# A fused convolution and gated MLP in fp32: four of six block pairs in the Strassen form instead of three, with a new order of all engines

## The chip, the cores and the metric

The kernel runs on one core of one Trainium2 chip. The core has a matrix engine (TensorE, PE in the profile, with its weight loads shown apart as PEld), three engines for elementwise work (VectorE or DVE, ScalarE or ACT, GpSimd or POOL), a sync engine (SyncE or SP) that here only issues DMAs, and 16 DMA engines that move data between the memory of the chip (HBM) and the on-chip memory. ACT issues DMAs too, on a queue of its own. Each engine runs its own list of instructions in order, and waits for the others through semaphores. The matrix engine writes into eight accumulation banks (PSUM). The metric is the time of one execution in microseconds (us); lower is better.

## The reference

The input is x, 8 sequences of 4096 tokens with 192 channels, in fp32. First comes a causal depthwise convolution with 7 taps. The taps are shared by the channels of a head (8 heads of 24 channels) and normalised by a softmax. Its output is the input of an MLP:

```python
rms = np.sqrt(np.mean(x * x, axis=-1, keepdims=True) + 1e-06)
xn = x / rms * rms_g
g = xn @ w_gate                              # 32768 x 192 @ 192 x 1536
val = xn @ w_val                             # 32768 x 192 @ 192 x 1536
return (g / (1 + np.exp(-g)) * val) @ w_out  # 32768 x 1536 @ 1536 x 192
```

Nearly all arithmetic lies in the three matrix products.

## The kernel before

**Tiling.** The 32768 tokens are cut into 32 pairs of 2 x 512 tokens (`PAIRS`, T = 512). The 1536 inner channels are 12 blocks of 128, taken two at a time as block pairs j = 0 to 5 (`NP`). The 192 input channels are three thirds of 64 rows. One matmul uses half of the PE rows: the gate product runs in one half while the value product runs in the other.

**Gate and value products.** For one block pair and one token pair there are four results, a to d (2 token tiles x 2 blocks). In the plain form each is the sum of three thirds, called A, B and E, so 12 products (Aa, Ba, Ea, Ab and so on). In the Strassen form the first two thirds are taken as a 2 x 2 x 2 product with seven multiplications (P1 to P7), and the last third adds Q1 to Q4: 11 products. The tuple `FORM` says which block pairs use which. Each product is three matmul passes, for operands cut into a high part, a low part and a combination, times two halves, so six matmuls of 512 columns (line 899). The seven Strassen products need additions between them. These are done on the banks: f1 copies bank a, when it holds P1 alone, to bank b; f3 copies P5 from bank c to a buffer; f4 adds the buffer to bank b and writes c; f5 adds it to b after P7 and writes d. The copies are at lines 667 (ACT) and 669 (DVE), the adds at line 967 (DVE). So P6 and P2 wait for f1; P7, Q2 and P3 wait for f4; Q4, Q3 and P4 wait for f5.

**Silu and multiply.** When a result is complete, ACT takes the silu of the gate half into a buffer (ga to gd, line 973), and DVE multiplies it with the value half into a tile (ma to md, line 980). Then the double bank is free again; there are four of them. `open` takes the next free one.

**Output product.** It too is a Strassen form, over all six block pairs: seven multiplications o1 to o7, one step per block pair (o1.0 to o7.5, 42 steps, line 923). They add up in three banks X, Y and Z; o1 starts X, o7 starts Z, Y is a copy of X (c1). The sums h1 to h4 of the multiplied tiles (line 950, DVE or POOL) feed o5, o7, o6 and o3. At the end DVE and ACT combine the banks (s7, c2, C21, C22) and transpose them (T11 to T22, line 938), and stores go out (st, line 1022).

**The next tokens.** Beside this work the tokens of the following pairs are made ready: loads (ld, line 146), seven taps (cv0 on ACT, cv1 to cv6 on DVE, line 435), square, reduction, factor, spread and scaling (sq, red, pow, bc, mul; pow and mul on POOL), eight puts into a scratch in HBM (pl, line 1033), six fetches from it with the channels across partitions (ft, line 631), sums for the Strassen form (x1 to x4, line 827) and the cuts into parts (n, l, d, lines 667, 813 and 815).

**Weights.** The parts of the weights lie in HBM (`wd`) and are loaded into a ring of ten slots, one piece of 192 KB at a time (line 785, from SP). A plain block pair needs six pieces, a Strassen one nine. When the last product that uses a piece is written down, `ring_load` loads the next piece into its slot.

**What sets the order.** The order is written out by hand as words; no scheduler changes it. `LINE` lists the PE steps of one token pair (a word such as P1.0 is product P1 of block pair 0). `ORDER` lists, for one window, what all engines are told: `p3` is the next three PE steps, `Vma.0` is DVE doing ma of block pair 0; the first letter is the engine (A, V, G for POOL, S for SP). A `+` means the next token pair, `++` the one after, `-` the one before. `FIRST` is the window of token pair 1, which still uses unsplit weights, with the preparation of the split weights (W) beside it. The last lines of the function run them:

```python
run([w for row in FIRST for w in row.split()], 1)
for w in range(2, PAIRS + 1):
    run([w for row in ORDER for w in row.split()], w)
```

Of the kernel before, what the change touches and what calls it, by code (L numbers as in the profile page):

```python
# [1323 lines left out]
```

## Time and profile before

| | us |
|---|---|
| three runs | 2497.64, 2503.84, 2503.82 (median 2503.82) |
| the profiled execution | 2498.01 |
| its span, first to last instruction | 2496.2 |
| PE busy | 2477.4 (99%) |
| DVE busy | 2013.4 (81%) |
| ACT busy | 926.6 (37%) |
| POOL busy | 852.5 (34%) |
| gate products, line 899 | 12420 matmuls, 1442.9 busy |
| adds f4 and f5, line 967 | 180, 1229 ns each |
| silus, line 973 | 744, 598 ns each |
| multiplies, line 980 | 744, 684 ns each |
| ring loads, line 785 | 1350 of 192 KB |
| HBM | 349.26 MB read, 58.39 MB written |

The profile is one execution. A row gives the line, the engine, the operation and its tiles, then the busy time. An idle time before an instruction is put down to what ended it. The ends of matmuls are modelled, so that a busy PE can still have short pauses between steps. The chain that ended last follows the work back from the last instruction: at each step to what released it, or to the instruction before it on its engine. The two kinds of stretches of one token pair look different: in a stretch of gate products (828.23 to 872.19) the DMA engines are busy at 0.81 and move 212 GB/s, and DVE is busy 33.76 of 43.96 us; in a stretch of output steps (872.19 to 896.90) it is 0.48, 108 GB/s, and 21.85 of 24.71 us. The granted PE clock is 1.00 in both.

### The profile page before, as it was taken

How to read it: one execution, taken by the hardware profiler on the slowest of the kernel's cores; microseconds unless marked ns; L12 is line 12 of the kernel's file. 1: busy time of each engine (PE TensorE's matmuls, PEld its weight loads, DVE VectorE, ACT ScalarE, POOL GpSimd, SP SyncE). 2: the span in 40 equal slices, each digit the busy share in tenths (PEclk: the TensorE clock that was granted, in tenths of full speed). 3: DMA queues.
4: the chain of work that ended last, by engine and by line, in shares of the span. 5: the costliest groups of instructions: out<-in, count | busy, mean ns of one | idle time of the engine just before them, and what ended most of it. 6: DMA issues, size and time to landing. Idle time of an engine off the chain costs nothing.

```text
span 2496.2 us, 69094 instructions
## 1 busy us (share of the span) xinstructions
PE 2477.4 (99%) x29140; PEld 1932.4 (77%) x29140; DVE 2013.4 (81%) x2482; ACT 926.6 (37%) x1349; POOL 852.5 (34%) x640
## 2 busy tenths in 40 slices
PE   8999999999999999999999999999999999999999
PEld 5647778877777787777877788777777877778887
DVE  8668888788878788878888788888787888888864
ACT  6443334333333333333333343333333333333331
POOL 0553333423243324343333333233433233333331
PEclk9999999999999999999999999999999999999999
DMA  7365667766678666677666677666686666786652
GB/s 150 59 189 152 155 170 192 173 180 157 156 171 205 169 166 158 160 180 193 172 160 157 168 192 176 179 154 157 170 201 172 165 158 162 181 197 171 159 140 81
DMA packets 701735, 412.22 MB, mean 165 GB/s; under 512 B 506610, under 2 KB 687730, under 8 KB 701426
## 3 DMA queue, kind: packets, MB, share of 16 engines
q1 hardware_dynamic: 540176, 353.65, 56.1%
q10 hardware_dynamic: 161250, 54.16, 9.7%
q8 instruction: 230, 3.77, 0.6%
q14 instruction: 79, 0.65, 0.1%
HBM read 349.26 MB, written 58.39 MB: 163 GB/s over the span
## 4 chain that ended last, share of the span: by engine, by line
PE 96%; DMA 2%; SPq 1%; DVE 0%; ACT 0%; issue 0%; ACTq 0%; DVEq 0%
PE ps L899 56%; PE ps L923 34%; PE ps L871 2%; PE ps L1070 2%; DMA xb<-xd 1%; PE ps L1111 1%; SPq L146 0%; SPq L229 0%; DMA ht<-in_moe_w_gate_dram 0%; DMA x<-in_x_dram 0%; DMA ht<-in_moe_w_val_dram 0%; ACT tt L973 0%; DVE ht L980 0%; SPq L631 0%; ACT o_sb L1119 0%
## 5 line engine op out<-in xcount | busy, mean ns | idle before, releaser
L899 PE MATMUL ps<-part,ring 64*128 64x512 f32 x12420 | 1442.9, 389 | 0.0
L899 PEld LDWEIGHTS ps<-part,ring 64*128 64x128 f32 x12420 | 1185.8, 184 | 236.5 <-issue 18.0
L973 ACT ACTIVATE tt<-ps 128x512 f32<-128x512 f32 x744 | 430.9, 598 | 726.4 <-PE ps L899 586.4
L980 DVE TENSOR_TENSOR ht<-ps,tt 128x512 f32<-128x512 f32 x744 | 495.5, 684 | 190.5 <-ACT tt L973 185.3
L923 PE MATMUL ps<-ht,wo_sb 128*32 128x384 f32 (+2 forms) x6696 | 443.1, 380 | 3.3 <-DVE ht L980 3.3
L923 PE MATMUL ps<-ht,x 128*32 128x256 f32 (+2 forms) x6696 | 441.9, 379 | 0.0
L950 POOL TENSOR_TENSOR ht<-ht 128x512 f32<-128x512 f32 x186 | 283.7, 1538 | 433.3 <-PE ps L923 377.1
L950 POOL TENSOR_TENSOR hs<-ht 128x512 f32<-128x512 f32 x93 | 120.2, 1293 | 834.2 <-DVE ht L980 832.3
L923 PEld LDWEIGHTS ps<-ht,wo_sb 128*32 128x32 f32 x6696 | 296.2, 110 | 121.9 <-issue 21.5
L923 PEld LDWEIGHTS ps<-ht,x 128*32 128x32 f32 x6696 | 302.5, 110 | 90.6
L435 DVE SCALAR_TENSOR_TENSOR y<-xh,tp,y 128x1536 f32<-128x1536 f32 x186 | 342.5, 1841 | 1.3
L667 ACT COPY ps<-ps 128x384 f32<-128x384 f32 (+1 forms) x121 | 104.1, 860 | 408.7 <-PE ps L899 311.7
L967 DVE TENSOR_TENSOR ps<-ps,tt 128x1024 f32<-128x1024 f32 x180 | 221.3, 1229 | 42.1 <-PE ps L899 35.0
L667 ACT COPY tt<-ps 128x384 f32<-128x384 f32 (+1 forms) x122 | 91.0, 746 | 227.0 <-PE ps L923 207.8
L923 PE MATMUL ps<-hs,x 128*32 128x128 f32 (+2 forms) x2232 | 161.0, 379 | 0.0
L950 DVE TENSOR_TENSOR ht<-ht 128x512 f32<-128x512 f32 x186 | 126.5, 693 | 8.0 <-POOL hs L950 4.6
L923 PEld LDWEIGHTS ps<-hs,x 128*32 128x32 f32 x2232 | 108.9, 110 | 27.7
L667 ACT CAST part<-xb 128x1024 fp32r<-128x1024 f32 x87 | 91.3, 1050 | 104.0 <-DMA xb<-xd 67.1
L950 DVE TENSOR_TENSOR ht<-hs,ht 128x512 f32<-128x512 f32 x155 | 122.4, 806 | 2.9 <-PE ps L923 1.1
L950 DVE TENSOR_TENSOR hs<-ht 128x512 f32<-128x512 f32 x93 | 116.4, 1252 | 2.1
L815 DVE SCALAR_TENSOR_TENSOR part<-part,xb 128x1024 fp32r<-128x1024 f32 x87 | 105.5, 1213 | 0.0
L813 DVE TENSOR_TENSOR part<-xb,part 128x1024 fp32r<-128x1024 f32 x87 | 105.4, 1212 | 0.0
(136 smaller groups left out, 1460.1 us busy)
## 6 DMA issues: line engine op xcount, KB each, us to landing
ring<-wd SPq DMA_DIRECT2D x1350, 192.0 KB
xb<-xd SPq DMA_DIRECT2D x122, 256.0 KB
xd<-xh ACTq DMA_DIRECT2D x240, 96.0 KB
xh<-in_x_dram SPq DMA_DIRECT2D x192, 105.0 KB
xb<-xd ACTq DMA_DIRECT2D x58, 256.0 KB
out_dram<-o_sb ACTq DMA_DIRECT2D x93, 96.0 KB
wd<-part SPq DMA_DIRECT2D x5, 1152.0 KB
xh<-in_x_dram SPq DMA_DIRECT2D x56, 98.4 KB
```

The source lines that it names most:

```text
L435: nc.vector.scalar_tensor_tensor(out=y, in0=xk, scalar=w, in1=y, op0=ALU.mult, op1=ALU.add)
L667: nc.scalar.copy(out=dst, in_=src)
L813: e.tensor_tensor(out=split_of(g, 1).bitcast(F32R), in0=src, in1=high, op=ALU.subtract)
L815: nc.vector.scalar_tensor_tensor(out=split_of(g, 2).bitcast(F32R), in0=high, scalar=1.0 + SPLIT, in1=src, op0=ALU.mult, op1=ALU.subtract,)
L871: nc.tensor.matmul(out=self.both(j, c)[:, h, :], lhsT=wf[HALF[h], k, 2 * j + f, :], rhs=rb[HALF[h], k, g, :], start=(k == 0), stop=(k == K ...
L899: nc.tensor.matmul(out=self.both(j, c)[:, h, :], lhsT=left[HALF[h]], rhs=right[HALF[h]], start=(first and q == 0), stop=True, skip_group_c ...
L923: nc.tensor.matmul(out=self.acc(b)[i * Q : (i + 1) * Q, at : at + n], lhsT=left, rhs=cols, start=fresh, stop=True, skip_group_check=True, ...
L950: engine[eng].tensor_tensor(out=dst, in0=a, in1=b, op=op)
L967: nc.vector.tensor_tensor(out=self.both(j, c), in0=self.both(j, "b"), in1=s5, op=ALU.add)
L973: nc.scalar.activation(out=tt[:, t, :], in_=self.both(j, c)[:, 0, :], func=AF.Silu)
L980: nc.vector.tensor_tensor(out=self.hv(j, "abcd".index(c)), in0=self.both(j, c)[:, 1, :], in1=tt[:, t, :], op=ALU.mult,)
L1070: nc.tensor.matmul(out=bank(h, bks[h])[:], lhsT=wf[HALF[h], AT[h][k], u * NF + f, :], rhs=xb[HALF[h], g, k, :], start=(k == 0), stop=(k == ...
```

## The change

`FORM` becomes (0, 1, 1, 0, 1, 1): block pairs 1, 2, 4 and 5 are in the Strassen form, 0 and 3 plain (before: 0, 2 and 4 in the Strassen form). `LINE`, `ORDER` and `FIRST` are replaced. Per window there are 68 gate products for 69 and 48 ring loads for 45. Four f4 and four f5 stand for three each; f1 is three times on ACT and once on DVE (before three on ACT), f3 four times on ACT (before two on ACT, one on DVE). The eight puts and two of the six fetches move from ACT's queue to SP's. Between DVE and POOL some h sums, x3 and some l cuts change places. All PE steps of a token pair now lie in its own window, so that no step of two token pairs interleaves. No instruction changes in kind or size, and nothing outside of these four constants is edited; the lines below them move by three.

```diff
--- before.py
+++ after.py
@@ -68,46 +68,49 @@
     SPAN = 1509
     SPLIT = 2.0**-12
     HIGH = 0xFFFFF000
-    FORM = (1, 0, 1, 0, 1, 0)
+    FORM = (0, 1, 1, 0, 1, 1)
     PLAIN = tuple((j, c) for j in range(NP) for c in "abcd")
     ORDER = (
-        "Vd.0 An.4 An.3 Ac2- p5- Gh4.2- Vl.2 Vd.4 Vh4.3- Vl.3 Vd.3 Vl.0 Vd.2 Vh4.0- Vh4.5-",
-        "p8- Gh4.4- Gh4.1- VT11- VC22- p2- p1 Gl.4 Acv0+ Af1.0 VT22- VC21- p1- VT21- p3 Vcv1+",
-        "p1 Af3.0 Ast1.2- Vcv2+ Vf4.0 p3- p3 Aga.0 Ast1.0- Vcv3+ VT12- Vma.0 Sst0.2- Agc.0",
-        "Ast0.3- p1 Vf5.0 p2 Vcv4+ p1 Vmc.0 Vcv5+ p2 Sst1.3- p1 Sst0.4- Sst0.0- Agb.0 Ast1.1-",
-        "Agc.1 Ast0.1- Vmb.0 p2 Vcv6+ Agd.0 p2 Aga.1 Vmd.0 Vma.1 Vmc.1 p1 Asq+ Vred+ p1 Af1.2",
-        "Sst1.4- Gh1.0 Agb.1 Vmb.1 p1 Gpow+ p3 Af3.2 p1 Vf4.2 p4 Aga.2 Agd.1 Vma.2 Vbc+ Vf5.2",
-        "Gmul+ p1 Agc.2 p1 Apl.0+ Apl.1+ Apl.2+ p1 Vmd.1 Vmc.2 p6 Agd.2 Agb.2 Apl.3+ Vmb.2",
-        "Vmd.2 Apl.4+ p1 Agb.3 Aga.3 Apl.5+ p1 Vmb.3 Vma.3 p4 Af1.4 Vf3.4 Agc.3 Apl.6+ Apl.7+",
-        "p3 Vmc.3 p1 Vf4.4 p2 Aga.4 Gh1.1 p1 Agd.3 Aft.0+ Sft.2+ Vma.4 Vf5.4 Vh3.1 Sft.3+",
-        "Aft.1+ Sld.0++ Vmd.3 Sft.4+ Sld.1++ Sft.5+ Sld.2++ Sld.3++ Sld.4++ Sld.5++ Sld.6++",
-        "Sld.7++ p7 Gh1.3 Agc.4 Agd.4 Vmc.4 Vmd.4 Agb.4 p1 Vh1.2 Vh3.0 Vmb.4 p7 An.0+ p1",
-        "Aga.5 Agd.5 p1 Vh1.4 An.1+ Vx1+ Vmd.5 Vma.5 p1 Gh3.3 p2 Gh3.2 Agb.5 p2 Gh3.4 p2 Gx3+",
-        "Agc.5 Vd.1+ p1 Vh2.0 Vmc.5 Vh2.1 Vmb.5 Vh1.5 Vh2.2 Vh3.5 Vl.1+ Vh2.5 Vh2.4 Ac1 p1",
-        "Gx2+ An.2+ p6 Gh2.3 Gx4+ As7 p8",
+        "p2 Ast0.0- Sst0.4- Ast1.3- Sst0.2- Sst0.3- Sst1.4- p6 Sst0.1- Aga.0 Vma.0 Vcv4+ p3",
+        "Agc.0 Agd.0 Ast1.1- Vmc.0 p3 Vmd.0 Vcv5+ Ast1.0- Agb.3 Vmb.3 Af1.1 p2 Agb.0 Vcv6+",
+        "Vmb.0 p1 Af3.1 p3 Vf4.1 Aga.1 p2 Vma.1 p2 Vf5.1 p4 Asq+ Ast1.2- Aga.3 Vred+ Agd.1",
+        "Vmd.1 Vma.3 p1 Agc.1 Af1.2 p1 Agb.1 Vmc.1 p1 Gpow+ p1 Vbc+ Vmb.1 Gmul+ p1 Af3.2 p2",
+        "Spl.0+ Spl.1+ Aga.2 Vf4.2 p1 Spl.2+ Vma.2 p2 Vf5.2 p3 Spl.3+ Spl.4+ Agc.2 Agd.2",
+        "Spl.5+ Agb.2 Vmc.2 Vmd.2 p3 Vmb.2 Spl.6+ Spl.7+ Af1.4 p3 Agc.3 Af3.4 Vmc.3 p2 Aga.4",
+        "Vf4.4 Vma.4 p5 Sft.2+ Vf5.4 p1 Agd.3 Vmd.3 Sft.3+ Sft.0+ Sft.1+ p1 Agc.4 Vmc.4",
+        "Sft.4+ Sld.0++ Agd.4 Sft.5+ Sld.1++ Sld.2++ Sld.3++ Vmd.4 Sld.4++ Sld.5++ Sld.6++",
+        "Sld.7++ p3 Af3.5 Vf1.5 p1 Agb.4 Vf4.5 Vmb.4 p2 Aga.5 Vh1.4 Vma.5 p3 Gh1.1 Gh1.0",
+        "Gh1.2 Gh3.0 Gh1.3 Gh3.1 Gh3.3 Vf5.5 p3 Vh2.3 Vh3.2 Vh2.2 Gh3.4 p3 An.0+ Agb.5 Agd.5",
+        "Vx1+ p2 Vx3+ Vmd.5 Gx2+ Vl.0+ Vh2.4 Vmb.5 p1 Vh1.5 Vh3.5 p4 Agc.5 Ac1 An.1+ An.2+",
+        "An.3+ Gx4+ Gh2.1 p9 Vmc.5 Vh2.5 As7 An.4+ p2 Vh2.0 Vd.3+ Gl.2+ p3 Ac2 p4 Acv0++ p2",
+        "Gh4.1 Gh4.2 Gl.1+ Vh4.0 Vh4.5 Vd.4+ Vd.2+ Vl.3+ Vh4.4 Vh4.3 p6 Vl.4+ VT11 Vd.1+ VC22",
+        "Vd.0+ VC21 VT22 VT21 Vcv1++ p6 VT12 Vcv2++ Vcv3++",
     )
     FIRST = (
         "p1 Vcv5+ W p2 Vcv6+ p1 Aga.0 Vma.0 p2 Asq+ W W p1 Agb.0 W Vmb.0 W p1 Vred+ p2 Agc.0",
-        "Vmc.0 W p1 Gpow+ W W W p1 W p1 Agd.0 W Vmd.0 p1 Vbc+ Gh1.0 p1 Gmul+ p1 Aga.1 Vh3.0 W",
-        "Vma.1 p1 W W W W p1 W p1 Agb.1 Apl.0+ Vmb.1 p1 Apl.1+ p1 Apl.2+ W p1 Agc.1 Apl.3+ W",
-        "W W Vmc.1 Apl.4+ p1 W W Apl.5+ p1 Apl.6+ p1 Agd.1 Apl.7+ Vmd.1 p1 Gh1.1 W p1 W W W",
-        "p1 Aga.2 Vh3.1 W Vma.2 W p3 Agb.2 Vmb.2 W p1 W W W p1 W p1 Agc.2 W Vmc.2 p3 Agd.2 W",
-        "Vmd.2 p1 W W W Vh1.2 W p1 W p1 Aga.3 Gh3.2 Vma.3 p2 W p1 Agb.3 W W W Vmb.3 p1 W W p1",
-        "Aft.0+ p1 Aft.1+ Agc.3 Sft.2+ Vmc.3 p1 Sft.3+ W p1 Sft.4+ W W W Sft.5+ p1 Agd.3 W",
+        "Vmc.0 W p1 Gpow+ W W W p1 W p1 Agd.0 W Vmd.0 p1 Vbc+ Gh1.0 p1 Gmul+ p1 Aga.1 Gh3.0 W",
+        "Vma.1 p1 W W W W p1 W p1 Agb.1 Spl.0+ Vmb.1 p1 Spl.1+ p1 Spl.2+ W p1 Agc.1 Spl.3+ W",
+        "W W Vmc.1 Spl.4+ p1 W W Spl.5+ p1 Spl.6+ p1 Agd.1 Spl.7+ Vmd.1 p1 Gh1.1 W p1 W W W",
+        "p1 Aga.2 Gh3.1 W Vma.2 W p3 Agb.2 Vmb.2 W p1 W W W p1 W p1 Agc.2 W Vmc.2 p3 Agd.2 W",
+        "Vmd.2 p1 W W W Gh1.2 W p1 W p1 Aga.3 Vh3.2 Vma.3 p2 W p1 Agb.3 W W W Vmb.3 p1 W W p1",
+        "Sft.0+ p1 Sft.1+ Agc.3 Sft.2+ Vmc.3 p1 Sft.3+ W p1 Sft.4+ W W W Sft.5+ p1 Agd.3 W",
         "Vmd.3 W p1 Gh1.3 p2 Aga.4 Gh3.3 Vma.4 W p1 W W p1 W p1 Agb.4 W Vmb.4 p3 Agc.4 W",
-        "Vmc.4 p1 W p2 Agd.4 An.1+ Vmd.4 p1 Vx1+ Sld.0++ Vh1.4 p1 Gx3+ Vd.1+ p1 Aga.5 Gh3.4",
-        "Vma.5 Vl.1+ Sld.1++ p1 Gx2+ p1 An.2+ p1 Agb.5 Sld.2++ Gx4+ Vmb.5 p1 Sld.3++ p2 Agc.5",
-        "Sld.4++ Vmc.5 p1 Sld.5++ p1 Sld.6++ Agd.5 p1 An.0+ Vmd.5 p1 Vh2.0 Sld.7++ Vh1.5 p2",
-        "Gh2.3 Vh3.5 Vh2.5 p1 Vh2.1 p1 Vh2.4 p1 Ac1 Vh2.2 p2 R p7 As7 p7",
+        "Vmc.4 p1 W p2 Agd.4 Vx1+ Vmd.4 p1 Vx3+ Vh1.4 p1 Gx2+ p1 Aga.5 Gh3.4 Vma.5 An.1+",
+        "Sld.0++ p1 An.2+ p1 An.3+ p1 Agb.5 Sld.1++ Gx4+ Vmb.5 p1 An.4+ Sld.2++ p1 Vd.3+ p1",
+        "Gl.2+ Agc.5 Sld.3++ Vmc.5 Gl.1+ p1 Sld.4++ Vd.4+ p1 Vd.2+ Agd.5 Sld.5++ p1 Vl.3+",
+        "An.0+ Vl.0+ Vmd.5 Vd.0+ p1 Vh2.0 Sld.6++ Vl.4+ Vh1.5 p1 Vh2.3 Vd.1+ Sld.7++ p1 Vh3.5",
+        "Vh2.5 p1 Vh2.2 p1 Vh2.4 p3 Ac1 Gh2.1 R p3 Vh4.0 p1 Vh4.4 p1 Vh4.3 p1 Gh4.2 p5 As7 p1",
+        "Vh4.5 p4 Ac2 p2 Acv0++ p3 VT11 Gh4.1 p5 VC22 p2 VC21 p3 Vcv1++ p2 VT12 VT22 VT21",
+        "Vcv2++ Vcv3++",
     )
     LINE = (
-        "P1.0 P5.0 P6.0 P2.0 Q1.0 P7.0 P3.0 Q2.0 Ac.1 Q4.0 Q3.0 P4.0 Bc.1 Ec.1 Aa.1 Ba.1 Ea.1",
-        "Ab.1 Eb.1 P1.2 Bb.1 P5.2 P6.2 P2.2 Q1.2 Ad.1 Ed.1 P7.2 P3.2 Bd.1 Q2.2 Q3.2 Q4.2 Aa.3",
-        "Ba.3 P4.2 Ea.3 Ab.3 Bb.3 Eb.3 Ac.3 Bc.3 P1.4 P5.4 Ec.3 P6.4 P2.4 Q1.4 Ad.3 Bd.3 P7.4",
-        "Ed.3 Q2.4 P3.4 Q4.4 P4.4 Ad.5 Q3.4 Ed.5 Aa.5 Ea.5 Ab.5 Bd.5 Ac.5 Bc.5 Ba.5 Bb.5 Ec.5",
-        "Eb.5 o1.0 o1.5 o1.3 o1.1 o1.4 o1.2 o7.0 o7.3 o7.4 o2.0 o7.1 o7.2 o2.5 o6.0 o7.5 o6.2",
-        "o2.3 o6.1 o2.4 o6.4 o6.3 o6.5 o4.4 o2.1 o4.1 o5.0 o2.2 o5.5 o4.3 o5.3 o4.5 o5.2 o5.4",
-        "o5.1 o4.2 o4.0 o3.5 o3.2 o3.3 o3.1 o3.4 o3.0",
+        "Aa.0 Ea.0 Ad.0 Ac.0 Ba.0 Ed.0 Bd.0 Ec.0 Bc.0 Ab.3 P1.1 Bb.3 Eb.3 Ab.0 Eb.0 Bb.0 P5.1",
+        "P6.1 P2.1 Q1.1 Aa.3 P7.1 Ba.3 Ea.3 Q4.1 P3.1 Q2.1 Q3.1 P1.2 P4.1 P5.2 P6.2 P2.2 Q1.2",
+        "Ac.3 P7.2 Q2.2 P3.2 Q4.2 P4.2 Q3.2 P1.4 Ec.3 Bc.3 P2.4 P5.4 P6.4 Q1.4 Ad.3 Ed.3 P7.4",
+        "Bd.3 Q2.4 P3.4 Q4.4 P1.5 P4.4 P5.5 Q3.4 P6.5 P2.5 Q1.5 Q2.5 P7.5 o1.0 o1.3 o1.5 o1.2",
+        "Q3.5 Q4.5 P4.5 P3.5 o1.4 o7.0 o7.1 o1.1 o7.4 o7.2 o2.0 o2.4 o2.3 o2.2 o7.3 o6.1 o6.4",
+        "o6.2 o7.5 o2.5 o6.3 o4.0 o6.0 o6.5 o4.5 o4.4 o5.2 o5.3 o2.1 o4.1 o5.4 o5.5 o5.1 o5.0",
+        "o4.3 o4.2 o3.0 o3.4 o3.3 o3.1 o3.5 o3.2",
     )
 
     cst = ctx.enter_context(tc.tile_pool(name="cst", bufs=1))
```

## The prediction

> **What bounds the kernel now.** I read the page's busy row first, then the chain that ended last, one window of that chain in order of time, and only then the groups, the waits and the timeline of the engines that feed TensorE (PE).
>
> ```profile
> PE 2477.4 (99%) x29140; PEld 1932.4 (77%) x29140; DVE 2013.4 (81%) x2482; ACT 926.6 (37%) x1349; POOL 852.5 (34%) x640
> PE 96%; DMA 2%; SPq 1%; DVE 0%; ACT 0%; issue 0%; ACTq 0%; DVEq 0%
> ```
>
> PE is the bound, and 96% of the chain is PE following PE. But a busy share of 99% cannot show a stall of some tenths of a us, so I measure PE by the pace of its steps. One window of the chain (columns: start, length, what):
>
> ```profile
> 752.65 44.03 PE ps L899 x381
> 796.68 24.84 PE ps L923 x304
> 821.52 0.89 PE ps L899 x6
> 822.41 0.79 PE ps L923 x8
> 823.20 2.94 PE ps L899 x24
> 826.14 2.09 PE ps L923 x24
> ```
>
> These six runs are one token pair: 64, 1 and 4 gate products (6 matmuls each) and 38, 1 and 3 output steps (8 rows each). A gate product costs (44.03 - 0.89) / 63 = 0.685 us, and 0.89 - 0.685 = 0.205 us is paid once per run. An output step costs (24.84 - 0.79) / 37 = 0.650 us, and 0.14 once per run. The other runs fit: 4 x 0.685 + 0.205 = 2.945 against 2.94, 3 x 0.65 + 0.14 = 2.09. So a window is 75.58 us, and no stall above 0.1 us hides in it. It happens 30 times (12420 / 414 gate matmuls): 2267 of the 2496 us.
>
> The rows that decide what a shorter round trip costs (timeline; the wait before it in brackets) and the two waits of the weight loads:
>
> ```profile
> 844.38 1.23 DVE L967 TENSOR_TENSOR ps<-ps,tt 128x1024 f32<-128x1024 f32 x1 [0.43 <-PE ps L899]
> 854.58 1.00 ACT L667 COPY ps<-ps 128x1024 f32<-128x1024 f32 x1 [0.95 <-PE ps L899]
> 870.26 1.09 ACT L973 ACTIVATE tt<-ps 128x512 f32<-128x512 f32 x2 [0.76 <-PE ps L899]
> 871.38 1.29 DVE L980 TENSOR_TENSOR ht<-ps,tt 128x512 f32<-128x512 f32 x2 [1.38 <-ACT tt L973]
> ...
> PEld ps L899 <- DVE ht L980: 6.4, 30, 0.2
> PEld ps L899 <- ACT ps L667: 4.8, 30, 0.3
> ```
>
> The ACT copy at 854.58 is f1 of block pair 4. Between P1.4, which it reads, and P6.4, which needs it, stand two products, 2 x 0.685 = 1.37 us. The copy takes 1.00, and the next weight load waits about 0.16 us for it (4.8 / 30) without PE losing pace. So both hand-overs together (PE to the copy, the copy to PE) take at most 1.37 - 1.00 = 0.37 us. The DVE add at 844.38 starts 0.20 after the product it waits for by the pace above (23 products after 828.23 + 0.205, 844.19), and the multiply that starts at 871.38 ends near 872.06, the output step that needs it starts at 872.19, 0.12 later. So both together are 0.32 to 0.37 us. Two products are thus enough for a copy on ACT, and just so; the old order never gives a DVE add fewer than three (P7.4 Ed.3 Q2.4 P3.4 Q4.4).
>
> **The change part by part.** The sum is made against the profiled execution, 2498.01 us (span 2496.2, 1.8 around it). The three timed runs are 2497.64, 2503.84 and 2503.82, so it lies 5.8 us below their median.
>
> 1. Four pairs in the Strassen form: 4 x 11 + 2 x 12 = 68 products instead of 69, output steps stay 42. Saves 0.685 x 30 = 20.5 us, on the path because PE is the path.
>
> 2. Fewer runs. The new line goes 64 products (all but the last four), four output steps (o1.0 o1.3 o1.5 o1.2), four products (Q3.5 Q4.5 P4.5 P3.5), 38 steps, and the windows no longer interleave: two runs of each kind instead of three. Saves (0.205 + 0.14) x 30 = 10.3 us.
>
> 3. Three DVE adds now have only two products between what they read and what needs them: P7.1 Ba.3 Ea.3 Q4.1, P7.2 Q2.2 P3.2 Q4.2, P6.5 P2.5 Q1.5 Q2.5. The add takes 1.23 (its 180 rows lie at 1.23), with hand-overs 1.55 to 1.60, against 1.37: a stall of 0.18 to 0.23 even with DVE idle before it. Lower end 0.10 (the smallest hand-overs that fit these rows, 0.20 + 0.04); I take 0.20, as the weight load of the ACT copy shows almost no reserve. 3 x 0.20 x 30 = 18 us (9 to 21).
>
> 4. The first step of the second output sum. o7.0 opens the bank that held d of pair 5 and must wait for multiply md.5. PE does Q4.5, P4.5, P3.5, o1.4, o7.0. ACT has gb.5 ahead of gd.5, and gb.5 needs P4.5. From the end of P4.5: hand-over 0.12 to 0.20, two silus 1.09, 0.03 to the multiply, 0.68, 0.12 to PE: 2.07. PE has P3.5, a run change and o1.4 to do: 0.685 + 0.14 + 0.65 = 1.475. Stall 0.60, x 30 = 18 us. Lower end 0.5. Upper end 1.1: x1 and x3 stand on DVE ahead of md.5 and wait for the fetched tokens; in the trace x1 waits 1.87 us a window (54.2 / 29). I stay at 0.60: the fetch is issued about 10 us earlier in the gate phase than before.
>
> 5. Smaller ones: f1.5 is now on DVE (a copy of this size took 1.23 there) behind md.4, with three products to run in; md.1 stands behind the 2.2 us reduction. Together 0.1 a window, 3 us (0 to 9).
>
> 6. Other engines. DVE gains two adds (2.46), one split of a token sum (1.21) and x3 (1.22), loses one h1 (1.25) and two splits of fetched tokens (2.42), trades one h3 for one h4: +1.2 us in 75, to about 83% busy, hidden by the PE time beside it except at 3 to 5. POOL +1.9 (h1 1.29 and h3 1.54 in, h4 1.54 and x3 1.74 out, one more split of 2.38), ACT two more copies (2.0) and ten DMA issues fewer: both below half busy, no cost. If that cover went, the o-phase of DVE (21.85 busy of 24.71 before) would be first.
>
> 7. SP. Eight puts and two fetches move from ACT's queue to SP, and three more weight pieces are loaded (48 for 45, 30 x 3 x 192 KB = 17 MB on 412). In the old line the shortest time between a freed ring slot and its use is six products, 4.1 us, without a wait for it; in the new line it is seven (4.8), and eight (5.5) where puts stand between, two ahead of one load at most at 0.59 us each in the trace: 5.5 - 1.2 = 4.3. I cost it at nothing; without that margin every late load stalls PE one for one.
>
> 8. The ends. All ten stores of the last pair now stand behind the last transpose; in the trace eight stores took 6.72 us on ACT's queue and about half of these had started before. +3 us (0 to 5). The start moves the same puts behind the weight writes of SP: 0, from -4 to +4.
>
> Sum: 2498.0 - 20.5 - 10.3 + 18 + 18 + 3 + 3 = 2509.2 against the profiled 2498.0, that is +11. Counted from the median it is 2515; the runs of before fall at both levels, so I forecast the middle, **2512 us**.
>
> The page "DMA: Bandwidth & Descriptors" of the Trainium skill (Anatomy of one DMA) gives about 2.0 us plus bytes over 436 GB/s; a ring piece would land in an estimated 2.5 us. By it, part 7 keeps an estimated 1.8 us (4.3 - 2.5) and rival B would have half its chance, with the sum as it is; the trace bounds the landing only from above, at 4.1 us.
>
> **The rivals.**
>
> A. The gain stands, other side: the round trip of DVE is shorter than I say, or PE takes up the waits in its queue as it did the 0.16 us of the copy, and parts 3 and 5 go to nothing, while the wait at o7.0 is at most 0.2. For it: PE lost no pace at the copy. Against: the add is 0.23 longer than the copy. Then 2498 - 30.8 + 3 + 0 to 6 = 2470 to 2477; it turns at 1.02 us of stalls a window, and up to there the result stays below 2501. Chance 0.26, with mixed cases up to 2492.
>
> B. SP becomes the bound: the puts wait for the normalisation on POOL, and ring loads behind them come late. For it: DMA engines are at 0.81 in the gate phase. Against: part 7. One us late at one place of each window adds 30 us: 2540. Chance 0.12.
>
> C. The granted clock falls because PE now pauses five times a window. The stretches of this trace show a granted clock of 1.00, the last one (2380 to 2496) 0.98; 2% on 30 x 74.6 us is 45 us: 2555. Against: no pause is above 1.1 us. Chance 0.03. The Trainium skill, "TensorE: Matmul & The Clock Gate", A second HAM failure mode, says that short pauses between groups of matmuls can make the gate swing; this trace has no such pauses and can't show it.
>
> My forecast (stalls of 1.0 to 1.9 us a window) has 0.59 and a range of its own of 2500 to 2530.
>
> **How the numbers follow.** About 0.3% (7.5 us) can be told from no change here. The forecast's 0.59 gives 0.46 slower and 0.13 same; A gives 0.23 faster and 0.03 same; B and C are slower, 0.15. Faster 0.23, same 0.16, slower 0.61. The range of 8 in 10 cuts the lowest part of A and the far part of B and C: 2476 to 2536.
>
> **What would show it.** In the chain, runs of 64, 4, 4 and 38, a first run longer than 44.03 by about 0.7 us, and the run that starts with o1.4 longer than 24.84 by 0.6. In the waits, weight loads of L902 waiting for the DVE add at L970 about 90 times, and loads of L926 for the multiply at L983 about 0.6 us or more 30 times. Waits for ring loads would mean B; a first run near 44.0 would mean A. The part I am least sure of is 4: were the bank free earlier, 18 us go.

## The result: 56 us slower, and where the time is

The changed kernel takes 2559.61 us (median of four runs, 2559.06 to 2561.63); the kernel before took 2503.32 beside it. The ratio is 1.0232, with a 95% interval of 1.0214 to 1.0249. The forecast was 2512, in a range of 2476 to 2536: the direction was right, the size was not. The profiled execution took 2559.58 us, its span is 2557.8.

The busy row and the chain of the changed kernel's page, which answer to the two lines shown of the kernel before:

```profile
PE 2496.4 (98%) x28960; PEld 1921.2 (75%) x28960; DVE 2114.0 (83%) x2511; ACT 989.8 (39%) x1409; POOL 957.6 (37%) x671
PE 86%; DVE 5%; DMA 3%; ACT 2%; issue 2%; POOL 1%; SPq 1%; ACTq 0%; DVEq 0%; POOLq 0%
```

PE still is the bound, but its share of the chain falls from 96% to 86%: the other engines now stand on the path. One window of the chain (start, length, what; "issue" is time in which nothing in the profile explains the wait):

```profile
1006.21 16.73 PE ps L902 x144
1022.94 0.14 issue
1023.08 9.89 PE ps L902 x84
1032.97 0.13 issue
1033.10 14.62 PE ps L902 x126
1047.72 0.13 issue
1047.86 2.33 PE ps L902 x18
...
1050.20 1.65 PE ps L902 x10
1051.85 2.75 PE ps L926 x32
1054.60 2.29 PE ps L902 x16
...
1056.96 1.09 ACT tt L976 x2
...
1058.08 0.70 DVE ht L983
...
1058.92 24.26 PE ps L926 x296
```

The runs of 64, 4, 4 and 38 are there, but the 64 products are cut into 24, 14, 21, 3 and 2. What each piece takes beyond 0.685 us a product (and 0.205 for the change of kind at the start) shows what the cuts cost: 0.23, 0.43, 0.37, 0.28 and 0.28, together 1.59 us, or 0.40 for each of the four cuts if all of it is put down to them. The cuts lie ahead of Q4.1, Q4.2, P6.5 and Q2.5. After the four products, the silus and the multiply lead to o7.0: from 1054.60 to 1058.92 it is 4.32 us, against 3.735 for the work of PE in it, a pause of 0.59, and the run of 37 steps behind it takes 0.21 more than 37 x 0.65. So the window is 76.96 us, 2.4 above 74.55, what 68 products, 42 steps and two changes of kind each way cost without a pause.

Between the two profiled spans lie 61.6 us: 30 windows of 77.16 on average instead of 75.73 (42.9; most are 77.0 and 75.6), a start that is 15.9 longer (below), and 2.6 at the end (8.2 instead of 5.6 us behind the last transpose).

### The profile page after: what moved, and what is told of

Same layout as the page of the kernel before. It is cut to its first block, busy times and chain, and to the rows that moved or that the text cites. A ratio compares the mean times of both kernels' runs of the same rounds, so it can differ in the third digit from the quotient of the medians.

```text
span 2557.8 us, 69178 instructions
## 1 busy us (share of the span) xinstructions
PE 2496.4 (98%) x28960; PEld 1921.2 (75%) x28960; DVE 2114.0 (83%) x2511; ACT 989.8 (39%) x1409; POOL 957.6 (37%) x671
## 4 chain that ended last, share of the span: by engine, by line
PE 86%; DVE 5%; DMA 3%; ACT 2%; issue 2%; POOL 1%; SPq 1%; ACTq 0%; DVEq 0%; POOLq 0%
PE ps L902 54%; PE ps L926 31%; ACT tt L976 1%; DVE ht L983 1%; DMA ring<-wd 1%; PE ps L1114 1%; DMA wd<-part 1%; DVE y L438 1%; DVE part L816 1%; DMA ht<-in_moe_w_gate_dram 0%; DVE ht L953 0%; POOL part L765 0%; SPq L232 0%; DVE ht L1091 0%; DMA xb<-xd 0%
## 5 line engine op out<-in xcount | busy, mean ns | idle before, releaser
L926 PE MATMUL ps<-ht,x 128*32 128x384 f32 (+2 forms) x6696 | 410.3, 381 | 22.9 <-DVE ht L983 15.4
L926 PE MATMUL ps<-ht,wo_sb 128*32 128x256 f32 (+2 forms) x6696 | 414.8, 380 | 2.2 <-ACT ps L670 1.9
L970 DVE TENSOR_TENSOR ps<-ps,tt 128x1024 f32<-128x1024 f32 x240 | 295.7, 1232 | 100.9 <-PE ps L902 51.3
L670 ACT COPY tt<-ps 128x384 f32<-128x384 f32 (+1 forms) x182 | 151.9, 835 | 245.7 <-PE ps L926 177.3
L953 POOL TENSOR_TENSOR hs<-ht 128x512 f32<-128x512 f32 x124 | 158.7, 1293 | 220.5 <-DVE ht L983 220.5
L816 POOL TENSOR_TENSOR part<-xb,part 128x1024 fp32r<-128x1024 f32 x58 | 169.6, 2925 | 49.1 <-ACT part L670 49.1
L953 DVE TENSOR_TENSOR ht<-hs,ht 128x512 f32<-128x512 f32 x155 | 166.2, 1089 | 5.4 <-DVE ht L953 0.5
L926 PE MATMUL ps<-hs,x 128*32 128x384 f32 (+2 forms) x2232 | 138.2, 379 | 0.0
L818 DVE SCALAR_TENSOR_TENSOR part<-part,xb 128x1024 fp32r<-128x1024 f32 x87 | 130.7, 1502 | 0.0
L926 PEld LDWEIGHTS ps<-hs,x 128*32 128x32 f32 x2232 | 94.4, 110 | 33.5
```

The lines of the kernel that those rows point to most:

```text
L670: nc.scalar.copy(out=dst, in_=src)
L816: e.tensor_tensor(out=split_of(g, 1).bitcast(F32R), in0=src, in1=high, op=ALU.subtract)
L818: nc.vector.scalar_tensor_tensor(out=split_of(g, 2).bitcast(F32R), in0=high, scalar=1.0 + SPLIT, in1=src, op0=ALU.mult, op1=ALU.subtract,)
L926: nc.tensor.matmul(out=self.acc(b)[i * Q : (i + 1) * Q, at : at + n], lhsT=left, rhs=cols, start=fresh, stop=True, skip_group_check=True, ...
L953: engine[eng].tensor_tensor(out=dst, in0=a, in1=b, op=op)
L970: nc.vector.tensor_tensor(out=self.both(j, c), in0=self.both(j, "b"), in1=s5, op=ALU.add)
```

## The experiments

Each group of runs had the kernel before run beside it on the same chip (2500.8 to 2503.5 us). So ratios are compared; 0.001 is 2.5 us, and the changed kernel stands at 1.0232. The groups follow the questions, not the order in which they ran.

**What does one add with two products cost?** First in the kernel before, with one product moved (e8):

```diff
-        "Ed.3 Q2.4 P3.4 Q4.4 P4.4 ...
+        "Ed.3 Q2.4 Q4.4 P3.4 P4.4 ...
```

> The kernel before with P3.4 moved behind Q4.4: P7.4 Ed.3 Q2.4 Q4.4 P3.4 P4.4, so two products instead of three stand between P7.4 and Q4.4, which the DVE add f5.4 joins. Nothing else changes. Theory of part 3: one pause of 0.20 us in 30 windows, +6 us, 2509 us; at the size read in the changed kernel (0.23 to 0.28 us) +7 to +8.5, up to 2512; the first run of products goes from 44.03 to 44.23 to 44.31 us. Rival A (the round trip is short enough, TensorE's queue takes the wait up): no change, 2502 to 2505 us.

Measured: 2512.20 us, ratio 1.0040 (1.0027 to 1.0052), 10 us. The chain, one window:

```profile
2128.61 33.20 PE ps L899 x275
2161.81 0.07 issue
2161.88 11.19 PE ps L899 x96
```

and the timeline there (columns: start, length; the wait before it in brackets):

```profile
2160.49 1.23 DVE L967 TENSOR_TENSOR ps<-ps,tt 128x1024 f32<-128x1024 f32 x1 [0.72 <-PE ps L899]
...
2161.84 10.28 PEld L899 LDWEIGHTS ps<-part,ring 64*128 64x128 f32 x91 [0.46 <-ACT tt L973]
```

The 64 products take 44.46 us instead of 44.03: one such add costs 0.43 in this window, 0.40 in most (76.00 against 75.60), twice the 0.20 of part 3. The add waits for nothing but PE and ends at 2161.72; the weight load behind it starts 0.12 later, after a wait of 0.46 (put down to ACT, which was long done). Of these 0.46 PE shows only 0.07 as "issue": the rest is in the lengths of its runs. Then the same with a shorter add (e9, e10):

```diff
-                    out=self.both(j, c), in0=self.both(j, "b"), in1=s5, op=ALU.add
+                    out=self.both(j, c)[:, :, 0:n], in0=self.both(j, "b")[:, :, 0:n],
+                    in1=s5[:, :, 0:n], op=ALU.add,   # f5.4 alone: n = 448, then 384; the other columns are left out
```

> The run with the kernel before and only two products between P7.4 and Q4.4, and now the add f5.4 on DVE done on 896 of its 1024 columns (the other 128 of block pair 4's d are left out, so its result is not the reference's). The add takes 1.23 us for 1024 columns, so about 1.09 for 896. With all columns the window lost 0.40 us (76.00 against 75.60): the weight load of Q4.4 waited 0.46, about 0.2 of it before TensorE ran dry. Theory L (every tenth by which the add ends earlier is won back): window 75.86 to 75.88, about 2508 us.

> The same with the add on 768 of 1024 columns (256 of block pair 4's d are left out), about 0.95 us. TensorE's pause itself, 0.2 us, is then over. Theory L (loss and length of the add fall together, down to the last tenth): window 75.72 to 75.75, about 2504 to 2505 us. Theory R (a pause costs its own length and then a restart of about 0.2 us, as every change between products and output steps does, and both vanish when TensorE no longer runs dry): window 75.60 to 75.64, 2501 to 2503 us. Part 3 of the prediction (a pause of 0.20 and nothing else) has no place for a loss of 0.40 with the whole add.

Measured: 2507.63 us, ratio 1.0031 (1.0020 to 1.0043), and 2503.06 us, 1.0009 (1.0000 to 1.0018). The first run of products in the chain of the one (896) and of the other (768):

```profile
2047.27 44.30 PE ps L899 x384
```

```profile
1970.58 44.12 PE ps L899 x383
```

In the groups the add takes 1.230, 1.099 and 0.966 us for 1024, 896 and 768 columns; windows without other waits are 76.00, 75.85 and 75.68, so the loss is 0.40, 0.25 and 0.08. It falls by 0.15 to 0.17 for every 0.13 of the add. If it went on so, it would be gone at about 0.90; no run of this kernel went that far.

The starts of the single matmuls in the traces divide this loss (medians of 30 windows, against the kernel before). The first matmul of Q4.4 starts 0.24, 0.09 and 0.00 late, and in all three runs some 0.09 more is lost on the products right behind it; the small rest lies at the change to the output steps. So the late start falls with the add one to one, as theory L has it, and a smaller price behind it stays even where Q4.4 is not late, which neither theory has. The last window, 75.68, lies midway between them. Two products last 1.37, so the late starts give 1.37 + 0.24 - 1.23 = 0.38 and 1.37 + 0.09 - 1.10 = 0.36 for both hand-overs together, the upper end of what I read off.

Next the three adds of the changed kernel, all shortened to 640 columns (e16):

```diff
+                n = 320 if (act, j) in (("f5", 1), ("f5", 2), ("f4", 5)) else T
```

> The changed kernel with its three two-product adds (f5.1, f5.2, f4.5) done on 640 of 1024 columns, so 384 columns of these sums are left out: 0.83 us instead of 1.23, shorter than the 0.90 at which the loss in the kernel before was gone. Theory (the three adds are what part 3 of the prediction prices, at 0.40 each and not 0.20): window 77.0 to between 75.8 and 76.1, 30 x 0.9 to 1.2 us less, 2523 to 2533 us. Part 3 at its own price: 18 us less, 2541. Rival (the wait behind each takes the time over, as after the exchange of P3.1 and Q4.1): 2548 us or more.

Measured: 2533.84 us, ratio 1.0126 (1.0111 to 1.0141): 26 us less than the changed kernel. About half of the windows lie between 75.80 and 76.1. The gate products of one window in the chain:

```profile
1152.48 40.71 PE ps L902 x346
...
1193.32 3.70 PE ps L902 x30
```

The cuts ahead of Q4.1, Q4.2 and Q2.5 are gone, and only the one ahead of P6.5 stays. By the starts of the matmuls the 64 products take 1.07 less (median), 0.36 for each add, which would be 32 us; some of it is lost again elsewhere, most clearly ahead of o2.0 (0.26 a window on average, 0.15 in the changed kernel). So the adds are the largest piece of the loss. The next run (e7) gives one add a third product instead of shortening it:

```diff
-        ... Ea.3 Q4.1 P3.1 Q2.1
+        ... Ea.3 P3.1 Q4.1 Q2.1
```

> The changed kernel with P3.1 and Q4.1 exchanged in LINE, so that three products instead of two stand between P7.1 and Q4.1, which the DVE add f5.1 joins. Theory of part 3 (two products are too short for this add): the pause ahead of Q4.1 goes; at the 0.20 us forecast that is 6 us, at the 0.23 to 0.28 us that the changed kernel's chain shows 7 to 8 us: 2551 to 2554 us against 2559.6. Rival (the add is late because DVE is busy with something else, or the time comes back at the next wait, P5.2 or Q4.2): no change, 2557.5 to 2561.

Measured: 2560.21 us, ratio 1.0233 (1.0219 to 1.0247): nothing. Its chain:

```profile
777.75 14.02 PE ps L902 x120
...
793.29 1.23 DVE ps L970
794.52 1.66 DVE s L460
...
796.71 0.61 DVE ht L983
...
797.36 7.19 PE ps L902 x60
```

The pause ahead of Q4.1 is gone and a new one stands 28 products into the window, ahead of P1.2. P1.2 waits for a multiply (796.71) that stands on DVE behind the reduction of the squares (794.52 to 796.7). The earlier pause had covered this one. (In e16 P1.2 does not wait; there the add that DVE does ahead of the reduction is 0.4 shorter.) So the reduction was moved too (e12):

```diff
-        "... Aga.3 Vred+ Agd.1", "Vmd.1 Vma.3 p1 ...
+        "... Aga.3 Agd.1", "Vmd.1 Vma.3 Vred+ p1 ...
```

> The changed kernel with P3.1 ahead of Q4.1, as in the run that gained nothing, and the reduction of the next tokens' squares (2.1 us on DVE) behind multiplies md.1 and ma.3 instead of ahead of them. Theory (two waits in a row there: Q4.1 for the add, and 5 products on, P1.2 or its neighbour for the bank that md.1 gives back from behind the reduction; with only the first taken away the second grew by the same): now both go, the first 38 products run without a pause, window 77.0 to 76.5 or 76.6, 2544 to 2549 us. Rival (the later reduction makes the normalised tokens late on POOL and SP): 2557 us or more, with waits for fetched tokens.

Measured: 2637.47 us, ratio 1.0550 (1.0533 to 1.0568), most windows 79.1 to 80.6: 78 us worse, and not for late tokens as the rival had it. Its chain:

```profile
2012.27 1.67 DVE s L460
...
2014.83 1.65 POOL r L470
...
2016.93 0.04 DVE s L480
...
2017.10 0.65 DVE ht L983
2017.75 1.16 DVE ps L970
```

The spread of the factors (L480) waits on DVE for POOL's power, which needs the reduction; multiply mb.1 and add f4.2 stand behind it in DVE's order, and PE behind them. In the changed kernel the reduction is earlier and most of POOL's 2.4 us is hidden: DVE waits there 0.7 a window (20.0 us in 30 waits), in this run 1.8 (54.6). At its place in the changed kernel it holds P1.2 up as soon as the add no longer holds up Q4.1, and the later place costs more than both.

**The wait for o7.0.** First the order of two silus (e2), then that of DVE behind them (e6):

```diff
-        ... An.0+ Agb.5 Agd.5", "Vx1+ p2 Vx3+ Vmd.5 Gx2+ Vl.0+ Vh2.4 Vmb.5 p1 ...
+        ... An.0+ Agd.5 Agb.5", (as before)                                      # first run
+        ... An.0+ Agd.5 Agb.5", "Vx1+ p2 Vx3+ Vmd.5 Gx2+ Vmb.5 Vh2.4 Vl.0+ p1 ...  # second run
```

> The changed kernel with one pair of words swapped: ACT takes the silu gd.5 ahead of gb.5. Theory: the 0.60 us pause of PE at o7.0 in each window (823.55 to 827.89 takes 4.34 us for work of 3.74) comes from gd.5 standing behind gb.5, which waits for a later product. Expected: the pause goes, the run before it and the hand-over take 3.74 to 3.9 us, -0.45 to -0.6 us a window, 2542 to 2546. Rival: DVE, not ACT, sets it (x1 and x3 stand ahead of md.5 and end at 825.7, with the split behind them); then 0 to -0.2 us a window, 2554 to 2560.

Measured: 2549.07 us, ratio 1.0182 (1.0167 to 1.0197); most windows are 76.55 to 76.7. Its timeline shows what came next:

```profile
821.11 0.69 DVE L953 TENSOR_TENSOR ht<-hs,ht 128x512 f32<-128x512 f32 x1
...
825.64 2.14 POOL L830 TENSOR_TENSOR tt<-xb,tt 128x512 f32<-128x512 f32 x1
...
826.57 1.76 DVE L953 TENSOR_TENSOR ht<-hs,ht 128x512 f32<-128x512 f32 x1
...
828.25 0.68 DVE L983 TENSOR_TENSOR ht<-ps,tt 128x512 f32<-128x512 f32 x1
...
829.02 0.46 ACT L670 COPY ps<-ps 128x384 f32<-128x384 f32 x1 [3.08 <-DVE ht L983]
```

PE no longer stops for o7.0, but for o2.0, five steps later. Copy c1 (829.02) waits for the bank that mb.5 (828.25) gives back, and mb.5 stands on DVE behind split l.0 and sum h2.4. That sum takes 1.76 us beside POOL's x2 and 0.69 a moment earlier without it. (The 0.88 us that the next expectation gives for this pause counts one step too few. The four products and 38 steps take 28.29 us here and 27.78 without a pause, so it costs 0.5.)

> Silu gd.5 ahead of gb.5 on ACT as in the run before, and on DVE multiply mb.5 directly behind md.5, ahead of split l.0 and sum h2.4. Theory (after gd.5 was moved, o2.0 waits 0.88 us a window for copy c1, c1 for the bank that mb.5 gives back, and mb.5 stands behind 1.3 + 1.76 us of other DVE work): that pause goes too, the window goes from 76.55 to about 75.7, the kernel from 2549.1 to 2520 to 2528 us. Rival (the next late operation, h2.4 or a sum behind it, takes the pause over): window at 76.2 or more, 2538 to 2550 us.

Measured: 2539.10 us, ratio 1.0154 (1.0139 to 1.0170), the shortest windows are 76.15, the median is 76.5. The chain has the last 38 steps in one piece of 24.84 us again, as in the kernel before. Both pauses of the output steps are gone: four products and 38 steps take 27.79 instead of 28.58, which would be 24 us. 20 arrive; in eight windows PE now waits for the transposes of the pair before (3.8 us together). The second run gave 10 of them and not 25, for the reason told above.

**Copy f1.5 ahead of P6.5** (e3, e11).

```diff
-        "Sld.7++ p3 Af3.5 Vf1.5 p1 ...
+        "Sld.7++ p2 Af1.5 Af3.5 p2 ...   # first run; and in LINE: P5.5 P6.5 Q3.4 P2.5
+        "Sld.7++ p3 Af1.5 Af3.5 p1 ...   # second run; LINE untouched
```

> The changed kernel with the copy f1 of block pair 5 on ACT instead of DVE, ahead of f3, and P6.5 one product earlier (P5.5 P6.5 Q3.4 P2.5 Q1.5 Q2.5), so that the add f4.5 has three products to run in instead of two. Theory: P6.5 waits for the copy behind the multiply md.4 on DVE (about 0.3 us), and Q2.5 waits for the add with two products (0.285 us). Expected: both pauses go, -0.5 us a window, 2560 - 15 = 2545; the run of gate products takes 45.1 to 45.2 us instead of 45.67. Rival: the pace of the products itself is worse in this order (more changes of bank or weights that arrive late), so that the places of the waits do not matter: 0 to -0.1 us a window, 2557 to 2560.

Measured: 2562.03 us, ratio 1.0236 (1.0221 to 1.0251): nothing. The pause ahead of Q2.5 is gone, but with one product less ahead of P6.5 the copy is late again, now on ACT: the weight load of P6.5 waits 0.94 us for it, and the copy waits for the bank that md.4 gives back.

> The changed kernel with copy f1.5 on ACT ahead of f3.5 instead of on DVE; LINE is untouched. In the changed kernel f1.5 (1.23 us on DVE, behind md.4) ends 0.05 to 0.1 us too late for P6.5, and the window loses 0.37 us there (0.17 pause, 0.2 restart). Theory: on ACT the copy takes 1.00, ends 0.2 us earlier, the pause and the restart go: window 77.0 to 76.6 or 76.7, 2548 to 2552 us. Rival (f3.5 behind it on ACT makes the add f4.5 late, so that Q2.5 takes the time over): 2556 to 2562 us.

Measured: 2555.12 us, ratio 1.0219 (1.0204 to 1.0235). Most windows go to 76.55 to 76.8, and the chain shows 21 and 3 products in one piece (16.78 us): the cut ahead of P6.5 is gone. But a dozen windows of thirty are 77.0 to 78.1, and PE waits ten times for copy c1 ahead of the output steps (3.6 us together), in the changed kernel five times (1.9): 3 to 5 of some 11 us arrive.

**Puts on SP, rival B** (e1 in FIRST, e4 in ORDER).

```diff
-        "Spl.0+ Spl.1+ Aga.2 ... Spl.7+ ... Sft.0+ Sft.1+
+        "Apl.0+ Apl.1+ Aga.2 ... Apl.7+ ... Aft.0+ Aft.1+   # in FIRST, then in ORDER
```

> The changed kernel with one part undone: in the first window alone (the words of FIRST) the eight puts and the first two fetches go back to ACT's queue. Theory: in the first window SP holds the puts, which wait for the scaling on POOL, ahead of the writes of the split weights, so that the preparation of the weights runs late and PE stalls there; the windows start 15.9 us later than before the change. Expected: those 16 us come back, 2560 - 16 = 2544, and the 30 windows stay at 77.0 us. Rival: the start is late because token pair 2 is made ready earlier in the new first window and its work stands ahead of the multiplies on DVE; then nothing comes back (2557 to 2560).

Measured: 2559.0 us, ratio 1.0221 (1.0204 to 1.0238): no change.

> The changed kernel with the eight puts and two fetches of every later window (the words of ORDER) back on ACT's queue; the first window keeps them on SP. Theory: SP is not late for any ring load in the windows, so nothing is gained: 2556 to 2564 (ACT has ten DMA issues more, which may hold a silu for up to 0.1 us a window). Rival B of the prediction: the puts hold ring loads and these cost up to 0.8 us a window; then 2536 to 2550.

Measured: 2658.45 us, ratio 1.0620 (1.0604 to 1.0635), windows of 79.7 to 82.0. Neither the theory nor the rival had this. Its chain:

```profile
824.38 3.02 POOL xh L488
...
827.42 0.58 ACTq L1036
...
828.76 0.61 ACT tt L976
```

On ACT the puts wait for POOL's normalisation and hold the silus behind them, and PE stops for 2.1 us in each window (62.5 in 30 waits). In this order SP is the better place for them. The granted clock was 0.986 to 0.988 in all four executions, 0.997 or 0.998 in those of e1 to e3 on the same chip; so an estimated 25 of the 99 us (1.1% of 30 x 74.6) are the clock and not the wait itself.

**The start** (e5, e13, e18, e17). PE's timeline of the changed kernel has five pauses in pair 1; in the kernel before, the same products run from 129.04 to 191.1 without one (first row; then the changed kernel):

```profile
129.04 62.07 PE L871 MATMUL ps<-xb,part 64*128 64x512 f32 x288 [0.72 <-DVE o_sb L1123]
...
162.24 13.19 PE L874 MATMUL ps<-xb,part 64*128 64x512 f32 x60 [1.66 <-DVE ht L983]
176.45 5.42 PE L874 MATMUL ps<-xb,part 64*128 64x512 f32 x24 [1.02 <-DVE ht L983]
...
190.10 8.00 PE L874 MATMUL ps<-xb,part 64*128 64x512 f32 x36 [2.14 <-DVE ht L983]
...
216.02 3.71 PE L926 MATMUL ps<-ht,x 128*32 128x384 f32 x36 [7.39 <-DVE ht L953]
```

PE ends the steps of pair 1 at 234.6, against 222.6 with five products (3.8 us) of pair 2 already done. The longest pause came first:

```diff
-        "... An.4+ Sld.2++ p1 Vd.3+ p1", "Gl.2+ Agc.5 ... Gl.1+ ... Vd.4+ p1 Vd.2+ ... Vl.3+", ...
+        "Vh2.5 p1 Vh2.2 p1 Vh2.4 p3 Ac1 Gh2.1 Vd.3+ Gl.2+ Gl.1+ Vd.4+ Vd.2+ Vl.3+ Vl.0+ Vd.0+",
+        "Vl.4+ Vd.1+ R p3 Vh4.0 ...
```

> The changed kernel, only its FIRST row edited: the ten split operations of token pair 2 (eight on DVE, two on POOL) move behind the h sums of pair 1. Theory (DVE is strictly in order, and about 9.6 us of splits stand between 200 and 216 us ahead of h sums that the output steps wait for): the last output step of pair 1, which ends at 234.7 us, ends 8 to 13 us earlier, and the kernel goes from 2559.6 to 2547 to 2552 us; the steady window stays at 77.0. Rival (the start is late because of the weight preparation, whose chain runs on POOL and SP until 189 us): no change, 2557 to 2562.

Measured: 2554.15 us, ratio 1.0210 (1.0194 to 1.0225). The pause of 7.39 falls to 2.33 and the steps end at 229.4. That is 5 us, half of what was expected.

```diff
-        ... Aga.1 Gh3.0 ... Gh3.1 ... Gh1.2 ... Vh3.2     # and the splits as above
+        ... Aga.1 Vh3.0 ... Vh3.1 ... Vh1.2 ... Gh3.2
```

> The changed kernel with the splits in FIRST behind the h sums, as in the run that gained 5 us, and the h sums h3.0, h3.1, h1.2 of pair 1 back on DVE and h3.2 back on POOL, as in the kernel before. Theory: the four pauses of TensorE between 160 and 190 us (1.66, 1.02, 0.67, 2.14, together 5.5 us, each ended by a multiply on DVE) come from the sums that moved to POOL, where they stand ahead of the weight preparation's own subtractions, whose next step on DVE stands ahead of the multiply: with the sums back the pauses go, 2554.2 becomes 2547 to 2550 us. Rival (the pauses come from somewhere else, the conversion or the taps): 2553 to 2556 us.

Measured: 2553.01 us, ratio 1.0208 (1.0193 to 1.0223). The four early pauses go from 5.5 to 4.6 us: that was not it. The groups show what was. The preparation of the weights, in the kernel before and in the changed one:

```profile
L758 DVE SCALAR_TENSOR_TENSOR part<-part 128x768 f32<-128x768 f32 x5 | 4.8, 957 | 1.4 <-ACT part L756 1.1
```

```profile
L761 DVE SCALAR_TENSOR_TENSOR part<-part 128x768 f32<-128x768 f32 x9 | 12.0, 1333 | 2.9 <-ACT part L759 2.3
```

`blocks()` gives a slice of the pairs in the Strassen form, and all six where they are not evenly spaced. Pairs 0, 2, 4 were; 1, 2, 4, 5 are not. So nine of ten preparation steps are 768 wide instead of five. The sentence in the section on the change that no instruction changes in size is wrong there.

```diff
-        if len(step) > 1:
-            return slice(0, NP)
+        if kind == 1:
+            return slice(0, NP)      # the kernel before, made to prepare all six
```

> The kernel before with one line of blocks() changed, so that it prepares the Strassen sums of all six block pairs instead of the three that use them; 9 of 10 preparation steps are then 768 wide, as in the changed kernel. Nothing reads the added part. Theory: pair 1's products, which run without a pause from 129.6 to 191.0 us in the kernel before, get pauses of 3 to 7 us, and the kernel goes from 2502 to 2505 to 2509 us. Rival (hidden beside the products of pair 1): 2500 to 2504 us.

Measured: 2507.51 us, ratio 1.0031 (1.0018 to 1.0043), and its timeline gets the pauses:

```profile
165.63 18.50 PE L871 MATMUL ps<-xb,part 64*128 64x512 f32 x84 [2.63 <-DVE ht L980]
...
186.12 13.48 PE L871 MATMUL ps<-xb,part 64*128 64x512 f32 x60 [1.99 <-DVE ht L980]
```

```diff
+            return t.rearrange("p (a b) n -> p a b n", b=3)[:, :, 1:3]   # pairs 1, 2, 4, 5
```

> The run with splits late and h sums back in FIRST, and now blocks() and prepare() make the Strassen sums of the weights for the four block pairs that use them (1, 2, 4, 5) and not for all six: 512 columns instead of 768 in each step, two shorter weight writes instead of one. Theory (the change of FORM makes blocks() return all six pairs, because 1, 2, 4, 5 are not evenly spaced; 9 of the 10 preparation steps are 768 wide instead of 5, the steps on DVE and POOL take 39 and 43 us instead of 14 and 18 with 768-wide ones slowed, and multiplies of pair 1 wait behind them): the three pauses of TensorE between 160 and 190 us (4.6 us together) fall below 3, 2553.0 becomes 2548 to 2551 us. Rival (the preparation is hidden): 2552 to 2555 us.

(The 39 and 43 us in it are a slip: in the groups the preparation takes 21.9 us on DVE and 24.9 on POOL, against 14.4 and 18.4.) Measured: 2550.96 us, ratio 1.0203 (1.0188 to 1.0218). In the trace the three pauses fall from 4.6 to 0.3 us and the steps of pair 1 end at 223.75 instead of 228.85, 5.1 earlier than in e13; the medians show 1 to 2 us less, within their spread.

**POOL beside DVE** (e15).

```diff
-        "... Vmd.5 Gx2+ Vl.0+ ...", "An.3+ Gx4+ Gh2.1
+        "... Vmd.5 Vx2+ Vl.0+ ...", "An.3+ Vx4+ Gh2.1
```

> The changed kernel with token sums x2 and x4 on DVE instead of POOL. It is about what a POOL operation costs a DVE operation beside it: in the trace an h sum of two SBUF operands takes 0.61 to 0.69 us on DVE while POOL is idle and 1.76 beside the token sum x2 on POOL. Theory (POOL slows it): the mean of the h sums into ht on DVE falls from 1.09 to below 1.00 us, the token sums on DVE take 0.6 to 0.7 us each, and DVE's whole busy time rises by less than 30 us although 60 operations were added; the kernel stays within 4 us of 2559.6, as these sums are not ahead of the wait for o7.0. Rival (the h sums are long for another reason): the mean stays at 1.05 to 1.10 and DVE's busy time rises by 36 us or more.

Measured: 2564.27 us, ratio 1.0247 (1.0230 to 1.0264). Two groups of the changed kernel, then the same two of this run (busy us, mean ns):

```profile
L953 DVE TENSOR_TENSOR ht<-hs,ht 128x512 f32<-128x512 f32 x155 | 166.2, 1089 | 5.4 <-DVE ht L953 0.5 <-PE ps L926 0.3
...
L816 DVE TENSOR_TENSOR part<-xb,part 128x1024 fp32r<-128x1024 f32 x29 | 50.6, 1744 | 0.0
```

```profile
L953 DVE TENSOR_TENSOR ht<-hs,ht 128x512 f32<-128x512 f32 x155 | 150.9, 989 | 4.9 <-DVE ht L953 0.5
...
L816 DVE TENSOR_TENSOR part<-xb,part 128x1024 fp32r<-128x1024 f32 x29 | 35.4, 1220 | 0.0
```

DVE took over 58 operations of 0.68 us (39.6 us) and its busy time rose by 4.9: the other 35 us are DVE operations that got shorter without POOL beside them, 30 of them in these two groups. The kernel gained nothing: the wait for o7.0 is as before (16.6 us in 29 waits, 15.4 in 28 in the changed kernel).

**All repairs that gained, together** (silus and mb.5, splits and h sums of FIRST, f1.5 on ACT, and the stores `st1` ahead of VT12; e14).

> The changed kernel with every repair that gained: gd.5 ahead of gb.5 and mb.5 behind md.5 (20.5 us), splits and h sums of FIRST (5 to 11), f1.5 on ACT (4.5 to 10), and the stores of the second half of a pair ahead of the last transpose of the first (up to 2.8 at the end). If these are separate losses they add up: 33 to 44 us, 2515 to 2527 us, still 15 to 25 above the kernel before, because the three two-product adds (0.40 us each, 36 us) stay. Rival (each repair only passes the wait on to the next engine queue): 2530 us or more.

Measured: 2526.18 us, ratio 1.0100 (1.0085 to 1.0115), a dozen windows of 75.8 to 75.9, the median 76.2. That is 33 us back, at the lower end of the sum. No version that was run beats the kernel before.

## Why the prediction was right in sign and wrong in size

The sum was 2509.2 for the profiled execution; it took 2559.58, 50.4 more.

1 and 2, fewer products and runs: right. The window without its pauses is 74.55, which is 75.58 - 1.03. (75.58 is a typical window of the kernel before; four of its 29 are 76.2 to 76.7.)

3, three adds with two products: the mechanism was right, the term was mis-sized. The three cuts cost 1.07 us a window, 32 us and not 18 (e16). The hand-overs were read off about right, 0.36 to 0.38 by the late starts in e8 and e9. The step that failed is the next one, which took "a stall of 0.18 to 0.23" for the whole price. In the changed kernel the three products start 0.20 to 0.29 late, and about 0.1 more is lost behind each; in e8 the 0.24 became 0.40. The term put the loss behind a late product at nothing, though the prediction charged 0.205 and 0.14 "once per run" where the kind of step changes. Why a late product costs more than its lateness stays open. The wait of 0.46 in e8 stands ahead of the weight load and only 0.07 of it shows on PE, which points at the weight load; no run tests it. This is 14 us of the miss.

4, o7.0: the pause is 0.59, forecast 0.60, and the waits name it.

```profile
PE ps L926 <- DVE ht L983: 15.4, 28, 0.6
...
PEld ps L902 <- DVE ps L970: 13.7, 34, 0.4
```

(The second row belongs to part 3: the prediction expected about 90 such waits, and the trace puts 34 down to the add. The lengths of the runs and e16 carry part 3, not this row.) The run behind o7.0 is 0.21 longer, which part 4 left out: 6 us. That undoing it calls up the next wait (o2.0) I had not said.

5, f1.5 on DVE: P6.5 waits for it, and as with the adds the cut costs 0.37, not 0.1: 8 us. md.1 behind the reduction, the other half of part 5, is hidden as long as Q4.1 is late.

6, other engines at no cost: wrong as a statement, small in price. DVE gained 100 us of busy time, 3.4 a window and not 1.2, as more of its operations run beside POOL's (the splits of x tokens, 1.74 us instead of 1.21). It reached PE only behind other waits (o2.0) and at the start.

7, SP at no cost: right within 4 us. Six weight loads waited for one of the 1440 ring pieces, 3.7 us together. The 2.5 us that the prediction gives for the landing of a piece is, in the Trainium skill, "DMA: Bandwidth & Descriptors" (Anatomy of one DMA), a fit for DMAs issued from GpSimd; the pieces are issued from SP, and no run here times their landing.

8, the ends: the tail took 2.6, forecast 3. The start took 15.9, forecast 0 within 4, and this step failed: I looked at the puts, which cost nothing (e1), and not at DVE's order in FIRST nor at `blocks()`, whose result hangs on FORM. Splits (5), preparation (5) and h sums (under 1) are 11 of the 16, and the pause that stays ahead of the h sums is 2.3. The changed kernel's own trace divides the 15.9 otherwise: 12.9 are the five pauses, 1.4 is what the 48 products of pair 1 take longer besides their four pauses (63.4 against 62.0 us), and some 1.5 is what the 26 output steps behind the long pause take longer than at 0.65 us each. For these steps the windows of the trace show a lower granted clock (stretch, length, busy time of PE, PEld, DVE, ACT and POOL, granted clock, DMA share and GB/s):

```profile
213.00:216.00 3.00, 0.00 (x0) 0.00 (x0) 2.90 (x6) 0.00 (x0) 0.49 (x1) 0.50 0.45 138
216.00:220.00 4.00, 3.98 (x46) 2.93 (x50) 2.84 (x3) 0.17 (x1) 1.09 (x1) 0.60 0.94 302
```

The granted clock is 0.50 and 0.60 here and 1.00 in the same stretches of the kernel before. No experiment undid this alone.

Together: 14 + 6 + 8 + 16 = 44 of the 50.4. Some 4 more (0.15 a window) are in the 1.59 that the pieces of the 64 products take beyond their pace, but at none of the four cuts (1.07 and 0.37).

The rivals: A (the gain stands) fell with e8, B with the six short waits for the ring; e4 can't decide B, since there ACT holds the silus up. C (the clock falls with many pauses) did not come in the windows: PE pauses five times in each of the 30, and the granted clock is 0.998. The Trainium skill, "TensorE: Matmul & The Clock Gate", A second HAM failure mode, says that short pauses between groups of matmuls can make the gate swing; here, with pauses of 0.1 to 0.6 us at five places of a window, it did not. With longer pauses the clock did fall: to 0.50 in the pause of 7.39 us at the start, and to a mean of 0.986 to 0.988 in e4, where PE stops for 2.1 us in each window. The range went up to 2536 for the bounds of the terms I had; part 3 reached only 21 us and part 8 only 4 at the start, and both came out above (32 and 15.9).
